# Warm-up matmuls on a preamble constant, and one weight block's load moved from the SP queue to the ACT queue

## The chip, the cores and the metric

The kernel runs on one core of a Trainium2 chip. The metric is the device time of one execution in microseconds (us); smaller is better. Times are medians of several executions. The profile adds one traced execution. Before the change the kernel takes 216.5 us, and most of that is one long stream of matmuls.

## The reference, cut to what matters

```python
def reference(A_x, ..., B_w1, B_b1, B_w2, B_b2, gate_w):
    x = A_x                                            # 2048 x 640, bf16
    g = _sigmoid((x * gate_w).sum(-1, keepdims=True))
    a = _A_ref(x, ...)                                 # a diagonal complex state-space scan
    b = _B_ref(x, B_w1, B_b1, B_w2, B_b2)              # gelu(x @ w1 + b1) @ w2 + b2; w1 is 640 x 1728
    return g * a + (1 - g) * b
```

The first work of TensorE (PE) is x @ w1 for the first 512 rows of x. It needs x transposed, 640 = 5 x 128 rows of it, and the five row blocks of w1. The five blocks are called k=0 to k=4 below.

## The kernel before

The kernel keeps a list of operations with priorities, and a small list scheduler turns them into one fixed order per engine. Loads are issued by the engine named in the call. `xtrans` is a transposing DMA (in this kernel only SP issues those), `w1load` a plain one of 128 rows of 2 KB.

```python
        w1load(0, "act", -101)
        xtrans(0, [0], 0, 1.27)          # x, block 0, transposed on the way in
        xtrans(0, [1, 2], 1, 1.27)       # blocks 1 and 2: "x's second transpose" below
        w1load(1, "sp", 2)               # "W1's second block" below: k=1
        w1load(2, "sp", 3)
        xtrans(0, [3, 4], 4, 1.27)
        w1load(3, "sp", 5)
        w1load(4, "sp", 6)
        ...
        # small parameter rows, 5 or 13 rows of 256 bytes, on ACT
        for i, (nm, (r0, src)) in enumerate(ROWS.items()):
            load(nm, "act", "l_" + nm, rows[r0:r0 + src.shape[0], :], src, [nm], prio=-100 + i, dur=0.4)
        load("b1b", "act", ..., prio=-96, dur=0.4)
        ...
        def f_warm():                    # dummy matmuls, so that PE's clock is up when the data comes
            t = None
            for _ in range(8):
                t = nc.tensor.matmul(PS[6][:, :], wz[:, 0:128], wz[:, :], start=True, stop=True)
            return inc("pe", t)
        op("warm", "pe", 3.2, ["wz"], [("bank", 6)], f_warm, prio=-1000)     # waits for a memset of wz by DVE
        ...
        def f_cols():                    # one PE transpose of the parameter rows
            return inc("pe", nc.tensor.transpose(psC, rows[:, :], ident[:, :]))
        op("cols", "pe", 0.3, list(ROWS) + ["b1b", "ident"], [("bank", 7)], f_cols, prio=7.5)
        ...
        def m1_first():                  # forty matmuls of 512 columns, k outermost: 8 column blocks for each k
            seq = [(k, jf) for k in range(KD) for jf in range(NW)]
            seq.remove((0, NW - 1))
            seq.insert(seq.index((1, NW - 1)), (0, NW - 1))
            for k, jf in seq:
                ... PS[jf] += W1sb[:, k, jf] ^T xT[0][:, k]     # reads ("xT", 0, k) and ("w1", k)
```

So PE does eight warm-up matmuls, seven matmuls of k=0, the transpose of the parameter rows, and then k=1, which needs x's second transpose and W1's second block.

Of the kernel before, what the change touches and what calls it, by code (L numbers as in the profile page):

```python
# [9 lines left out]
BF16 = mybir.dt.bfloat16  # L10
# [137 lines left out]
class Prog:  # L148
# [8 lines left out]
    def op(self, name, eng, dur, reads, writes, fn, prio=None, lat=0.0, after=()):  # L157
        deps = {}
        for k in reads:
            for w in self.last_w.get(k, ()):  # L160
                deps[w.idx] = w
        for k in writes:
            for w in self.last_w.get(k, ()):
                deps[w.idx] = w
            for r in self.last_r.get(k, ()):
                deps[r.idx] = r
        for a in after:
            deps[a.idx] = a
        deps = list(deps.values())
        E = self.E  # L170

        def run(eg, deps=deps, eng=eng, fn=fn):
            E.wait(eng, *[d.done for d in deps])
            return fn()

        it = self.sch.add(name, eng, dur, deps, run, prio=prio, lat=lat)
        for k in writes:
            self.last_w[k] = [it]
            self.last_r[k] = []
        for k in reads:  # L180
            self.last_r.setdefault(k, []).append(it)
        return it


def bass_gated_mix__ssm_conv_s5__dense_activation_gelu__prompt_kernel(
# [18 lines left out]
    _, S, D = A_x.shape  # L204
# [21 lines left out]
    with ExitStack() as es:  # L226

        def SB(name, shape, dt):
            return es.enter_context(nc.sbuf_tensor(name, list(shape), dt))
# [11 lines left out]
        cols = SB("cols", [128, 3 * KP + NF], FP32)  # L241
# [10 lines left out]
        ident = SB("ident", [128, 128], BF16)  # L252
# [33 lines left out]
        PS = [es.enter_context(nc.psum_tensor(f"ps{i}", [128, 512], FP32)) for i in range(8)]  # L286
# [13 lines left out]
        op = pr.op  # L300

        def inc(eng, ins):
            return E.inc(eng, ins, eng + "_s")
# [18 lines left out]
        def load(name, eng, sem, dst, src, writes, prio, dur=0.5, lat=2.5, reads=(), **kw):  # L322
            def fn():
                return dma_inc(eng, engines[eng].dma_start(dst, src), sem)
            return op(name, eng, dur, reads, writes, fn, prio=prio, lat=lat)
# [18 lines left out]
        def xtrans(q, ks, prio, dur):  # L344
            load_T(f"xT{q}_{ks[0]}", f"l_xT{q}_{ks[0]}", [(xT[q][:, ks[0]:ks[-1] + 1, :], x2[q * 512:(q + 1) * 512, ks[0] * 128:(ks[-1] + 1) * 128])],
                   [("xT", q, k) for k in ks], prio, dur)

        def w1load(k, eng, prio):
            load(f"w1_{k}", eng, f"l_w1{k}", W1sb[:, k, 0:FW], B_w1[k * 128:(k + 1) * 128, 0:FW], [("w1", k)], prio=prio, lat=2.6)
# [1 line left out]
        w1load(0, "act", -101)  # L351
        xtrans(0, [0], 0, 1.27)
        xtrans(0, [1, 2], 1, 1.27)
        w1load(1, "sp", 2)
        w1load(2, "sp", 3)
        xtrans(0, [3, 4], 4, 1.27)
        w1load(3, "sp", 5)
# [3 lines left out]
        ROWS = {"lre": (0, A_Lambda_re), "lim": (KP, A_Lambda_im), "ldt": (2 * KP, A_log_dt), "b1a": (3 * KP, B_b1[0:nmain])}  # L361
# [24 lines left out]

        op("const", "dve", 0.8, ["iota"], ["ident"], f_const, prio=-65)

        wz = SB("wz", [128, 512], BF16)

        def f_wz():
            return inc("dve", nc.vector.memset(wz[:, :], 0.0))  # L392

        op("wz", "dve", 0.35, (), ["wz"], f_wz, prio=-70)

        def f_warm():
            t = None
            for _ in range(8):
                t = nc.tensor.matmul(PS[6][:, :], wz[:, 0:128], wz[:, :], start=True, stop=True)  # L399
            return inc("pe", t)  # L400

        op("warm", "pe", 3.2, ["wz"], [("bank", 6)], f_warm, prio=-1000)

        def f_ones():
            inc("dve", nc.vector.memset(Gl[0][64:65, NF - 1, :], 1.0))
# [8 lines left out]
        def f_cols():  # L414
            return inc("pe", nc.tensor.transpose(psC, rows[:, :], ident[:, :]))  # L415

        op("cols", "pe", 0.3, list(ROWS) + ["b1b", "ident"], [("bank", 7)], f_cols, prio=7.5)

        def f_cols1():
            return inc("dve", nc.vector.tensor_copy(out=cols[:, :], in_=psC[:, 0:RT + 1]))  # L420
# [490 lines left out]
```

## Time and profile before

| | before |
|---|---|
| time, median of 3 (lowest to highest) | 216.51 us (216.29 to 216.52) |
| span of the profiled execution | 215.1 us |
| PE busy | 98% of the span |
| first warm-up matmul | 1.19 us |
| first matmul of k=0 / of k=1 | 4.58 / 7.57 us |
| last of the forty first matmuls starts | 14.71 us |

The page's first part gives the busy time of each engine, its share of the span, and the number of instructions.

```profile
PE 210.9 (98%) x1247; PEld 122.0 (57%) x1257; DVE 189.3 (88%) x262; ACT 99.0 (46%) x169; POOL 3.0 (1%) x11
```

PE is the limit, and its matmul work is fixed. A change can only gain or lose at the start, before the stream runs without a break. Here is PE's timeline of the first 17 us: start, length, engine, line, operation, tiles, and how many instructions the row merges. L399 is the warm-up, L601 the forty first matmuls, L415 the transpose of the parameter rows, L621 what follows.

```profile
1.19 3.60 PE L399 MATMUL ps<-wz 128*128 128x512 bf16 x8 [1.19 <-DVE wz L392]
4.58 2.89 PE L601 MATMUL ps<-xT,W1sb 128*128 128x512 bf16 x7
7.30 0.22 PE L415 MATMUL ps<-ident,rows 128*128 128x128 bf16 x1
7.57 7.52 PE L601 MATMUL ps<-xT,W1sb 128*128 128x512 bf16 x33
```

Seven matmuls of k=0 take 2.89 us and the next 33 take 7.52 us: starts are 0.427 us apart at first and 0.216 us apart later. PE starts at half its clock. (The page's row PEclk shows full clock from the first slice, so the half clock has to be read from this spacing; the trace's own clock record says full clock from 7.02 us.) The view of DMA issues, cut to the issues around 3.4 us, gives the time from issue to landing in its last column:

```profile
W1sb<-in_B_w_dram SPq DMA_DIRECT2D x1, 256.0 KB, 4.1
xT<-in_A_x_dram SPq DMA_TRANSPOSE x1, 3.8
```

W1's second block was issued at 3.40 us and landed at 7.48; x's second transpose was issued at 2.03 and landed at 5.83.

### The profile page before, as it was taken

The numbers are of one execution on the slowest core, as the hardware profiler recorded it, in microseconds if no ns is written. First come the engines' busy times: TensorE is split into PE (matmuls) and PEld (weight loads), VectorE is DVE, ScalarE is ACT, GpSimd is POOL, SyncE is SP. The second block draws the span as 40 slices with busy tenths as digits, with TensorE's granted clock in tenths as the row PEclk, the third lists the DMA queues.
The fourth block names the chain that finished last, engine by engine and source line by source line (L and its number), as shares of the span: only waits on it lengthen the run. The fifth ranks groups of instructions, "written<-read, shape, count | busy, mean of one in ns | idle before, by whom it ended". The sixth has DMA issues, their size and how long they took to land.

```text
span 215.1 us, 3184 instructions
## 1 busy us (share of the span) xinstructions
PE 210.9 (98%) x1247; PEld 122.0 (57%) x1257; DVE 189.3 (88%) x262; ACT 99.0 (46%) x169; POOL 3.0 (1%) x11
## 2 busy tenths in 40 slices
PE   7999999999999999999999999999999999999995
PEld 2344444444577775444467777444447777777773
DVE  3599999999999999999999999699999999959512
ACT  2469556675432224556642332556664233233220
POOL 1010000000000100000000010000000000000000
PEclk9999999999999999999999999999999999999999
DMA  6999799994000230100000022000000000000001
GB/s 132 293 274 200 196 382 227 215 216 101 0 0 34 43 140 0 34 0 0 3 0 30 0 84 103 30 3 0 0 0 3 8 35 21 30 30 30 34 30 30
DMA packets 30681, 16.09 MB, mean 75 GB/s; under 512 B 23948, under 2 KB 29772, under 8 KB 30668
## 3 DMA queue, kind: packets, MB, share of 16 engines
q1 hardware_dynamic: 30144, 14.32, 27.1%
q0 software_dynamic: 320, 1.31, 2.0%
q10 hardware_dynamic: 204, 0.27, 0.5%
q8 instruction: 10, 0.16, 0.3%
q14 instruction: 3, 0.02, 0.0%
HBM read 7.38 MB, written 2.62 MB: 47 GB/s over the span
## 4 chain that ended last, share of the span: by engine, by line
PE 98%; DVE 0%; issue 0%
PE ps L735 28%; PE ps L621 22%; PE ps L762 20%; PE ps L660 20%; PE ps L601 5%; PE ps L399 2%; PE ps L639 1%; DVE osb L795 0%; DVE wz L392 0%; PE ps L415 0%
## 5 line engine op out<-in xcount | busy, mean ns | idle before, releaser
L735 PE MATMUL ps<-W2sb,Gl 128*128 128x320 bf16 x448 | 63.6, 299 | 0.0
L735 PEld LDWEIGHTS ps<-W2sb,Gl 128*128 128x128 bf16 x448 | 43.8, 98 | 17.5
L621 PE MATMUL ps<-xT,W1sb 128*128 128x512 bf16 x214 | 47.3, 379 | 0.3
L762 PE MATMUL ps<-CT,H 128*128 128x320 bf16 x320 | 46.2, 299 | 0.0
L700 DVE TENSOR_TENSOR_SCAN W<-atab,V 128x1280 bf16<-128x1280 f32 x16 | 44.3, 2811 | 0.3
L660 PE MATMUL ps<-xT,BT 128*128 128x512 bf16 x196 | 43.1, 379 | 0.3 <-PE ps L639 0.2
L762 PEld LDWEIGHTS ps<-CT,H 128*128 128x128 bf16 x320 | 31.2, 98 | 12.6 <-issue 0.4
L743 ACT ACTIVATE E<-ps,g1col 128x320 bf16<-128x320 f32 x32 | 16.9, 527 | 43.8 <-PE ps L735 43.8
L628 ACT ACTIVATE Gl<-ps,cols 128x512 bf16<-128x512 f32 x44 | 29.8, 694 | 15.5 <-PE ps L621 15.5
L621 PEld LDWEIGHTS ps<-xT,W1sb 128*128 128x128 bf16 x220 | 21.5, 98 | 26.0
L660 PEld LDWEIGHTS ps<-xT,BT 128*128 128x128 bf16 x200 | 19.5, 98 | 23.5 <-issue 0.4
L669 ACT ACTIVATE U<-ps 128x512 bf16<-128x512 f32 x40 | 23.9, 597 | 18.3 <-PE ps L660 18.3
L773 ACT ACTIVATE E<-ps,gcol 128x320 bf16<-128x320 f32 x30 | 15.8, 527 | 24.2 <-PE ps L762 24.1
L465 DVE TENSOR_TENSOR osb<-xg,E 128x640 bf16<-128x640 bf16 x15 | 7.3, 486 | 9.0 <-ACT E L773 8.0
L781 DVE SCALAR_TENSOR_TENSOR xg<-xn,gcol,dsk 128x640 bf16<-128x640 bf16 x16 | 13.9, 883 | 0.4
L578 DVE SCALAR_TENSOR_TENSOR scr<-xn,gwb 128x640 bf16<-128x640 bf16 x16 | 13.2, 823 | 0.4
L465 DVE TENSOR_TENSOR V<-V,W 128x1280 bf16<-128x1280 bf16 x16 | 12.5, 821 | 0.3
L465 DVE TENSOR_TENSOR H<-H,V 128x1280 bf16<-128x1280 bf16 x16 | 12.5, 821 | 0.3
L465 DVE TENSOR_TENSOR V<-mr,U 128x2560 bf16<-128x2560 bf16 x8 | 11.9, 1489 | 0.2
L465 DVE TENSOR_TENSOR H<-c,W 128x2560 bf16<-128x2560 bf16 x8 | 11.9, 1490 | 0.1
L465 DVE TENSOR_TENSOR V<-s,W 128x2560 bf16<-128x2560 bf16 x8 | 11.9, 1485 | 0.0
L465 DVE TENSOR_TENSOR W<-mi,U 128x2560 bf16<-128x2560 bf16 x8 | 11.9, 1484 | 0.0
(77 smaller groups left out, 84.7 us busy)
## 6 DMA issues: line engine op xcount, KB each, us to landing
out_dram<-osb SPq DMA_DIRECT2D x15, 160.0 KB, 1.8
W2sb<-in_B_w_dram SPq DMA_DIRECT2D x1, 2080.0 KB, 11.1
xn<-in_A_x_dram SPq DMA_DIRECT2D x2, 640.0 KB, 6.0
xn<-in_A_x_dram POOLq DMA_DIRECT2D x2, 640.0 KB, 4.8
W1sb<-in_B_w_dram SPq DMA_DIRECT2D x4, 256.0 KB, 4.2
W1sb<-in_B_w_dram SPq DMA_DIRECT2D x1, 880.0 KB, 6.1
W1sb<-in_B_w_dram ACTq DMA_DIRECT2D x1, 256.0 KB, 2.7
gwb<-in_gate_w_dram SPq DMA_DIRECT2D x1, 160.0 KB, 5.6
```

The costliest lines, as they stand in the source:

```text
L465: return inc("dve", nc.vector.tensor_tensor(out=o, in0=a, in1=b, op=o_))
L578: t = inc("dve", nc.vector.scalar_tensor_tensor(out=scr[:, :], in0=xn[q % 2][:, c, :], scalar=1.0, in1=gwb[:, :], op0=ALU.mult, op1=ALU.mu ...
L621: t = nc.tensor.matmul(PS[bank][:, :], W1sb[:, k, jf * 128:(jf + 1) * 128], xT[q][:, k, :], start=(k == 0), stop=(k == KD - 1))
L628: return inc("act", nc.scalar.activation(Gl[q % 2][:, jf, :], PS[bank][:, :], ACT.Gelu_apprx_tanh, bias=b1col[:, jf:jf + 1]))
L660: t = nc.tensor.matmul(PS[bank][:, :], BT[:, ci, kd, k * 128:(k + 1) * 128], xT[q][:, kd, :], start=(kd == 0), stop=(kd == KD - 1))
L669: return inc("act", nc.scalar.activation(dst, src, ACT.Copy, scale=1.0 if ci == 0 else -1.0))
L700: t = inc("dve", nc.vector.tensor_tensor_scan(out=g[:, ci, :], data0=a, data1=v[:, ci, :], initial=0.0, op0=ALU.mult, op1=ALU.add))
L735: t = nc.tensor.matmul(PS[bank][:, 0:HALF], Gl[q % 2][0:n, jf, t4 * 128:(t4 + 1) * 128], W2sb[0:n, jf, cols], start=(jf == 0), stop=(jf == ...
L743: return inc("act", nc.scalar.activation(E1[c % NE][:, cols], PS[bank][:, 0:HALF], ACT.Copy, scale=g1col[:, c:c + 1]))
L762: t = nc.tensor.matmul(PS[bank][:, 0:HALF], H[b % NHB][:, ci, k, s * 128:(s + 1) * 128], CT[:, ci, k, cols], start=(i == 0), stop=(i == 2 ...
L773: return inc("act", nc.scalar.activation(E2[c % NE][:, cols], PS[bank][:, 0:HALF], ACT.Copy, scale=gcol[:, c:c + 1]))
L781: return inc("dve", nc.vector.scalar_tensor_tensor(out=xg[c % 2][:, :], in0=xn[q % 2][:, c % 4, :], scalar=gcol[:, c:c + 1], in1=dsk[:, :] ...
```

## The change

The intent: warm PE up earlier, and have W1's second block there earlier, so that the earlier clock can be used. The warm-up reads a constant that the preamble writes anyway, so it waits for no memset; nine matmuls fill the time that eight filled. W1's second block goes to the ACT queue, between the parameter rows. The two loads of b1's rows come later by that, so the transpose of the parameter rows is moved behind four more matmuls.

```diff
         w1load(0, "act", -101)
         xtrans(0, [0], 0, 1.27)
         xtrans(0, [1, 2], 1, 1.27)
-        w1load(1, "sp", 2)
+        w1load(1, "act", -97.5)
         w1load(2, "sp", 3)
...
-        wz = SB("wz", [128, 512], BF16)
-
-        def f_wz():
-            return inc("dve", nc.vector.memset(wz[:, :], 0.0))
-
-        op("wz", "dve", 0.35, (), ["wz"], f_wz, prio=-70)
+        one = nc.const_aps.tensor(1.0, [128, 1], BF16)

         def f_warm():
             t = None
-            for _ in range(8):
-                t = nc.tensor.matmul(PS[6][:, :], wz[:, 0:128], wz[:, :], start=True, stop=True)
+            for _ in range(9):
+                t = nc.tensor.matmul(PS[6][:, :], one.broadcast_to([128, 128]), one.broadcast_to([128, 512]), start=True, stop=True)
             return inc("pe", t)

-        op("warm", "pe", 3.2, ["wz"], [("bank", 6)], f_warm, prio=-1000)
+        op("warm", "pe", 3.6, (), [("bank", 6)], f_warm, prio=-1000)
...
-        op("cols", "pe", 0.3, list(ROWS) + ["b1b", "ident"], [("bank", 7)], f_cols, prio=7.5)
+        op("cols", "pe", 0.3, list(ROWS) + ["b1b", "ident"], [("bank", 7)], f_cols, prio=11.5)
```

## The prediction

> **What bounds the kernel.** TensorE. The chain of waits is 98% PE; after 9.5 us the timeline shows no PE wait above 0.2 us, only some missing records. The matmul work is fixed, so the change can only act on the first 15 us, until the fortieth W1 matmul of the first block is issued (14.7 us).
>
> **How that stretch goes now** (timeline, and the starts of single matmuls in the trace). The eight warm-up matmuls start at 1.19 us, behind a DVE memset (0.86 us, 0.27 long), and end at 4.6 us, just when the first transpose of x has landed (4.53). Matmuls with 512 columns start 0.427 us apart until about 7.02 us, then 0.216 us apart: half clock, then full clock. At 7.30 PE runs the transpose of the parameter rows, then waits about 0.2 us for W1's second row block (landed 7.48; k=1 starts 7.57). There is another 0.22 us wait at 9.3, within bank 7, which stays. The full-clock stretch in the trace lasts 208.21 us, from 7.02 to the end: 61.0 windows of 3.413 us. That agrees with the Trainium skill, "TensorE: Matmul & The Clock Gate", Part 1: the clock is judged in windows of 3.413 us and released after one busy window. On this grid the windows before are 0.20 to 3.61 and 3.61 to 7.02. The first had PE busy 2.42 of 3.41 us (71%, table by stretches), and did not release it.
>
> **What the change does.**
> 1. No memset to wait for: warm-up starts at about 0.78 us, 0.4 us earlier; nine at 0.427 still end at about 4.6. The first window is then 83% busy. If the threshold lies between 71% and 83%, full clock comes at 3.61 instead of 7.02. This is the whole question; I give it 60%.
> 2. W1's second block is issued by ACT at about 2.6 us instead of by SP at 3.40; I estimate landing near 6.0 instead of 7.48. SP's later loads are issued about 0.5 us earlier. b1's rows move 0.4 us later; the parameter transpose moves behind four more matmuls.
>
> **Critical path.** If released early: warm-up is over at 4.1, k=0 starts at 4.58 (x is the limit), takes 7 x 0.216, k=1 starts at about 6.2 when W1's second block is there, k=2 at 8.5, k=3 at 10.2 (W1's fourth block, 10.16 before, arrives a little earlier), the end of the forty at about 13.7 instead of 14.92. Gain about 1.2 us, time about 215.3. If not released early: only the 0.2 us wait for W1's second block goes, about 216.3. The DVE chain behind the parameter columns may start up to 0.9 us later, while PE gains; the tightest place is the second H tile (ready 71.1, read 74.1, 3 us of slack), so it shouldn't show.
>
> I set 215.5 us, range 214.9 to 216.5. Faster by over 2%: 0.01; within 2%: 0.97; slower: 0.02.
>
> **What would show it.** First warm-up matmul at 0.7 to 0.85 us. Spacing 0.216 us from about 3.6 us (released early) or from about 7.0 (not). A gap before the first W1 matmul in the first case. W1's second block landing before 6.5 us. k=1 starting without the 0.2 us wait. From the end of the forty matmuls on, the same timeline shifted by a constant.
>
> **What would make it wrong.** The windows may lie otherwise against the start of the kernel in other runs (the three times spread by only 0.23 us, so I take them as nearly fixed). Broadcast operands with step zero may be read more slowly than 0.427 us per matmul, and delay the first W1 matmul. The ACT-queue load shares DMA engines with the transposes of x and could delay them past 6.2 us. A later parameter transpose could hold up DVE more than I think.

## More of the kernel before

The next view gives, for stretches of 1 us, the length, the busy time of each engine with its count of instructions, the granted clock, the busy share of the 16 DMA engines (over 1 where packets are counted that end later) and GB/s.

```profile
4.00:5.00 1.00, 1.00 (x3) 0.16 (x2) 0.00 (x0) 1.00 (x1) 0.00 (x0) 1.00 1.28 230
5.00:6.00 1.00, 1.00 (x4) 0.44 (x3) 0.00 (x0) 0.01 (x1) 0.00 (x0) 1.00 0.66 178
6.00:7.00 1.00, 1.00 (x4) 0.31 (x3) 0.00 (x0) 0.00 (x0) 0.00 (x0) 1.00 0.94 333
7.00:8.00 1.00, 0.95 (x5) 0.32 (x4) 0.19 (x1) 0.21 (x1) 0.00 (x0) 1.00 1.28 131
8.00:9.00 1.00, 1.00 (x6) 0.49 (x5) 0.87 (x5) 0.68 (x2) 0.00 (x0) 1.00 1.23 290
```

## The result, and the profile after

The changed kernel is slower: 218.12 us (217.48 to 218.26, 4 runs) against 216.51 us (216.29 to 216.86). The ratio is 1.0067, with a 95% interval of 1.0043 to 1.0091. A ratio here and below is the mean time of one kernel's runs over that of the other's of the same rounds, so it isn't quite the ratio of the quoted medians. Executions over 1.5% slower than the fastest of the same kernel are left out of the means. The loss is under 2%, but it is clear of the noise, and it lies outside the predicted range.

PE's timeline of the changed kernel; L394 is the warm-up, L596 the forty matmuls, L410 the parameter transpose:

```profile
0.78 4.00 PE L394 MATMUL ps<-const-bfloat16-1.0 128*128 128x512 bf16 x9 [0.78 <-PEq L891]
5.64 1.68 PE L596 MATMUL ps<-xT,W1sb 128*128 128x512 bf16 x7 [0.87 <-DMA xT<-in_A_x_dram]
9.04 1.04 PE L596 MATMUL ps<-xT,W1sb 128*128 128x512 bf16 x4 [1.72 <-DMA xT<-in_A_x_dram]
10.04 0.22 PE L410 MATMUL ps<-ident,rows 128*128 128x128 bf16 x1
10.09 6.65 PE L596 MATMUL ps<-xT,W1sb 128*128 128x512 bf16 x29
```

The warm-up half does what it was meant to: it starts at 0.78 us, its broadcast operands take the usual 0.427 us a matmul, and the seven matmuls of k=0 now take 1.68 us, at full clock. But PE waits twice for x, 0.87 us before k=0 and 1.72 us before k=1 by the busy times. k=1 starts at 9.04 us instead of 7.57, and the fortieth matmul at 16.36 instead of 14.71. That is 1.65 us later, and the spans differ by the same 1.65 us (216.73 and 215.08): after the forty matmuls nothing is gained or lost. The chain of work that ended last shows where it hangs, with start, length and what ran or was waited for:

```profile
2.03 6.97 DMA xT<-in_A_x_dram
9.00 0.05 issue
9.04 1.04 PE ps L596 x4
```

The landing times of the loads issued around 2.6 us:

```profile
W1sb<-in_B_w_dram ACTq DMA_DIRECT2D x1, 256.0 KB, 6.2
xT<-in_A_x_dram SPq DMA_TRANSPOSE x1, 7.0
```

W1's second block is issued 0.8 us earlier than before (2.62) and lands 1.3 us later (8.79). x's second transpose is issued at the same 2.03 us and takes 7.0 us instead of 3.8, landing at 9.00. The packet records of the traces show the same: its 1,024 packets of 256 bytes began between 3.48 and 5.08 us before, and between 3.49 and 8.26 us here. (x's first transpose is later too, 5.60 instead of 4.53, but k=0 is through by 7.3 us, long before k=1 can start.) And in the same stretches as before the DMA engines are as busy and move much less:

```profile
4.00:5.00 1.00, 0.78 (x2) 0.00 (x0) 0.00 (x0) 0.80 (x1) 0.00 (x0) 1.00 1.13 143
5.00:6.00 1.00, 0.36 (x2) 0.21 (x3) 0.00 (x0) 0.48 (x1) 0.00 (x0) 1.00 0.80 115
6.00:7.00 1.00, 1.00 (x7) 0.39 (x4) 0.00 (x0) 0.00 (x0) 0.00 (x0) 1.00 1.25 152
7.00:8.00 1.00, 0.33 (x2) 0.00 (x0) 0.00 (x0) 0.00 (x0) 0.00 (x0) 1.00 1.17 162
8.00:9.00 1.00, 0.00 (x0) 0.00 (x0) 0.00 (x0) 0.00 (x0) 0.00 (x0) 1.00 0.85 183
```

The last column sums to 755 KB in these 5 us, against 1162 KB before, though the mean busy share is 1.04 here and 1.08 before. From 4 to 8 us a packet of 2 KB (a row of W1) took 253 ns on the mean, against 109 ns before, and 84 ns where copies run alone (9.2 to 10.5 us before, 10.0 to 11.3 us in the changed kernel).

So the theory (A): rows of W1 on ACT's queue and transposes of x on SP's queue are now in the DMA engines together, and both crawl. The rivals: (B) the new warm-up costs something; (C) any W1 block on ACT costs this, whenever it is issued; (D) the DMA engines are simply full, so only bytes count; (E) it is the changed order on SP; (F) SP and ACT share something in the making of descriptors (the orders that the DMA engines work from), rather than in the engines.

### The profile page after: what moved, and what is told of

Same layout as the page of the kernel before. It is cut to its first block, busy times and chain, and to the rows that moved or that the text cites. A ratio compares the mean times of both kernels' runs of the same rounds, so it can differ in the third digit from the quotient of the medians.

```text
span 216.7 us, 3195 instructions
## 1 busy us (share of the span) xinstructions
PE 211.0 (97%) x1258; PEld 121.7 (56%) x1258; DVE 188.8 (87%) x261; ACT 99.1 (46%) x169; POOL 3.0 (1%) x11
## 3 DMA queue, kind: packets, MB, share of 16 engines
HBM read 7.38 MB, written 2.62 MB: 46 GB/s over the span
## 4 chain that ended last, share of the span: by engine, by line
PE 95%; DMA 3%; SPq 1%; DVE 0%; issue 0%
PE ps L730 28%; PE ps L616 22%; PE ps L757 20%; PE ps L655 20%; PE ps L596 3%; DMA xT<-in_A_x_dram 3%; PE ps L634 1%; SPq L331 1%; DVE osb L790 0%; PE ps L410 0%
## 5 line engine op out<-in xcount | busy, mean ns | idle before, releaser
L616 PE MATMUL ps<-xT,W1sb 128*128 128x512 bf16 x220 | 48.1, 379 | 0.0
L655 PE MATMUL ps<-xT,BT 128*128 128x512 bf16 x200 | 43.8, 379 | 0.0
L596 PE MATMUL ps<-xT,W1sb 128*128 128x512 bf16 x40 | 9.3, 380 | 2.6 <-DMA xT<-in_A_x_dram 2.6
```

Source lines behind the costliest of these rows:

```text
L596: return inc("pe", nc.tensor.matmul(PS[jf][:, :], W1sb[:, k, jf * 128:(jf + 1) * 128], xT[0][:, k, :], start=(k == 0), stop=(k == KD - 1)))
L616: t = nc.tensor.matmul(PS[bank][:, :], W1sb[:, k, jf * 128:(jf + 1) * 128], xT[q][:, k, :], start=(k == 0), stop=(k == KD - 1))
L655: t = nc.tensor.matmul(PS[bank][:, :], BT[:, ci, kd, k * 128:(k + 1) * 128], xT[q][:, kd, :], start=(kd == 0), stop=(kd == KD - 1))
```

## The experiments

All kernels gave correct results. Times are us, with the number of runs. "SP-first" and other names are explained at their run.

### The two halves alone

The warm-up half alone, with W1's second block back on SP and the parameter transpose at its old place:

```diff
-        w1load(1, "act", -97.5)
+        w1load(1, "sp", 2)
...
-        op("cols", ..., prio=11.5)
+        op("cols", ..., prio=7.5)
```

> The warm-up half of the change alone: nine warm-up matmuls on the preamble's constant; W1's second row block stays on SP, the parameter transpose stays behind seven matmuls. Theory A (the loss is the ACT-queue load, which mixes with the transposes of x): x's second transpose lands near 5.8 us and W1's second block near 7.5 us as before, k=1 starts at 7.5 to 7.6 us whatever the clock does, and the time is that of before, 216.3 to 216.7 us. Theory B (the warm-up costs: broadcast operands, or ones, or the earlier start): about 218 us. What my prediction said of an early clock alone: up to 1.2 us faster; theory A says it is worth nothing here, since W1's second block is what k=1 waits for.

Measured: 216.5 (216.24 to 216.86, 6 runs), ratio 0.9998 (0.9978 to 1.0018). The warm-up neither costs nor gains, so B falls. Its timeline shows where an earlier start goes:

```profile
0.78 4.00 PE L394 MATMUL ps<-const-bfloat16-1.0 128*128 128x512 bf16 x9 [0.78 <-PEq L891]
4.75 2.50 PE L596 MATMUL ps<-xT,W1sb 128*128 128x512 bf16 x7
7.08 0.22 PE L410 MATMUL ps<-ident,rows 128*128 128x128 bf16 x1
7.79 7.52 PE L596 MATMUL ps<-xT,W1sb 128*128 128x512 bf16 x33 [0.48 <-issue]
```

PE is through k=0 and the parameter transpose a little earlier and then stands idle for 0.48 us, until W1's second block lands at 7.70. The slow clock of before had been hidden behind this load.

The load half alone: the diff's other lines on the old kernel, eight warm-up matmuls on the zeroed tile.

> The other half alone: W1's second block on ACT between the parameter rows, parameter transpose behind eleven matmuls; the old eight warm-up matmuls on the zeroed tile. Theory A: x's second transpose lands near 9.0 us and W1's second block near 8.8 us as in the changed kernel (5.8 and 7.5 before), k=1 starts near 9.0, time 217.5 to 218.3 us. Theory B: the time of before, about 216.5 us.

Measured: 216.93 in the middle of five runs, but these go from 215.68 to 218.58, and there was one execution of 791.71 us. Ratio 1.0023 (0.998 to 1.0066): inconclusive as a time. The profile fell on the execution of 791.71 us, in which matmuls of 512 columns are some 0.84 us apart to the end: PE at about a quarter of its clock, from the warm-up on (more on it at the end). Its loads are of use all the same: x's second transpose landed at 8.76 us and W1's second block at 8.51, as theory A said. The spread was not expected, and is taken up below.

### The suspected cost by itself

The warm-up half alone, plus a load on ACT of 256 KB that nothing computes with, at the very place where the changed kernel loads W1's second block. (The diffs here leave out one more line: a much later operation on ACT names the copy among its inputs.)

```diff
+        w1copy = SB("w1copy", [128, FW], BF16)
+        load("w1copy", "act", "l_w1copy", w1copy[:, :], B_w1[0:128, 0:FW], ["w1copy"], prio=-97.5, lat=2.6)
         w1load(1, "sp", 2)
...
-        op("cols", ..., prio=7.5)
+        op("cols", ..., prio=11.5)
```

> The suspected cost by itself: the kernel with the warm-up half alone (W1's second block on SP, behind x's second transpose, as before), but ACT also loads 256 KB of W1 that nothing computes with, at the place where the changed kernel loads W1's second block; parameter transpose behind eleven matmuls. Theory A: the idle copy alone delays x's second transpose from 5.7 to 8 to 9 us and the first by up to 1 us; W1's second block follows at about 9.5, k=1 starts at 9 to 9.8 us, time 217.5 to 218.7. Rival D (the DMA engines are full and only the bytes count): 256 KB are about 0.65 us of DMA at the 400 GB/s seen later, so W1's second block lands near 8.3 us and the time is at most 217.2. Rival E (what harms is the order on SP, W1's third block directly behind x's second transpose): no change, 216.5.

Measured: 219.32 (218.4 to 221.02, 6 runs), ratio 1.0135 (1.0102 to 1.0168), more than expected. The landing times of its loads issued at 3.4 us and of the transpose before them, and its DMA rates:

```profile
W1sb<-in_B_w_dram SPq DMA_DIRECT2D x1, 256.0 KB, 5.5
xT<-in_A_x_dram SPq DMA_TRANSPOSE x1, 6.4
```

```profile
4.00:5.00 1.00, 0.47 (x3) 0.11 (x2) 0.00 (x0) 0.80 (x1) 0.00 (x0) 1.00 1.06 193
5.00:6.00 1.00, 1.00 (x6) 0.49 (x5) 0.00 (x0) 0.48 (x1) 0.00 (x0) 1.00 1.05 92
6.00:7.00 1.00, 0.50 (x3) 0.00 (x1) 0.00 (x0) 0.00 (x0) 0.00 (x0) 1.00 1.14 113
```

The idle copy alone moves x's second transpose from 3.7 us after its issue (5.69, in the warm-up half alone) to 6.4 us after it (8.38). W1's second block, behind it on SP's queue, lands at 8.92, and k=1 starts at 9.01 us. SP's own order is that of before, so E falls. 256 KB at the 374 to 402 GB/s that these engines reach from 9 to 12 us in the kernel before are 0.7 us; the delay is 2.7 us, so D falls. Some of its runs are slower still. The slowest (221.02) has a mean granted clock of 0.984, so part of its excess is the clock; why was not traced.

Meant as the control: the same copy, issued by ACT at 8.6 us, so that it would run beside plain loads of SP only, with the parameter transpose at its old place.

```diff
-        load("w1copy", "act", ..., prio=-97.5, lat=2.6)
+        load("w1copy", "act", ..., prio=-948.5, lat=2.6, reads=["amag"])
```

> Control for the idle copy: the same 256 KB by ACT, but issued at about 8.6 us, when SP's ring holds plain loads of W1 (until about 12.5 us), parameter transpose behind seven matmuls. Theory A: copies beside copies cost only their bytes, W1's last loads land up to 0.7 us later (the remainder near 13.7 instead of 13.1, needed at 14.9), no matmul waits for them, time as with the warm-up half alone, 216.2 to 216.9 us. Rival (any second queue costs): a loss of 1 us or more.

Measured: 216.42 (216.3 to 216.92, 4 runs), ratio 1.0003 (0.9985 to 1.002). No matmul is delayed, so the expectation held for the time. But the run is not the control that it was meant to be. The first packet of the copy began only at 12.13 us, 3.5 us after the issue, when SP's plain loads were nearly through and the transposes of the next matrix (BT) had begun (11.97). The copy ran among those until 16.27 and landed at 16.76, and BT's landing moved from 16.82 us (warm-up half alone) to 20.12. Nothing needs that matrix so early. So this is a second case of a copy from ACT beside transposes from SP, with a delay of 3.3 us, and not a case of copies beside copies; for that see SP-first below. And the late first packet is a hint at F: what ACT issued did not start until what SP had issued earlier was under way.

### The same load at other times and from other queues

The changed kernel with W1's second block on ACT directly behind the first, at 1.19 us instead of 2.62:

```diff
-        w1load(1, "act", -97.5)
+        w1load(1, "act", -100.5)
```

> The changed kernel with W1's second block issued on ACT directly behind the first (at about 1.2 us instead of 2.6), before the parameter rows. Theory A: its packets run mostly from 2.5 to 4 us, against the first transpose of x; what is mixed is less, because both W1 blocks are mostly through before the second transpose begins. I expect the first transpose at 5 to 5.6 us, the second at 6 to 7, k=1 at 6.2 to 7.2 us, time 215.2 to 216.2. Rival C (any row block on ACT beside SP's transposes costs the same, whenever it is issued): about 218 us. If the parameter rows, now about 0.4 us later, were the limit, the parameter transpose would come after 10 us as in the changed kernel.

Measured: 215.87 (215.75 to 216.27, 6 runs), ratio 0.9971 (0.9953 to 0.999): a little faster than before. C falls: on the same queue, 1.4 us earlier, the load costs no time. x's first transpose landed at 5.30, W1's second block at 5.03, the second transpose at 6.23. The load's packets ran from 3.24 to 4.30 us, and for only 0.6 us of that beside packets of transposes (none ran from 3.66 to 4.13).

The changed kernel with W1's second block on SP in front of x's first transpose ("SP-first"):

```diff
-        w1load(1, "act", -97.5)
+        w1load(1, "sp", -1)
```

> The changed kernel with W1's second block issued on SP before the first transpose of x; nothing large is on the ACT queue beside transposes. Theory A: no mixing of packets of the two kinds over two queues; W1's second block lands before 4.5 us, the first transpose about 0.5 us later than before (5.1), the second near 6.4, k=1 at 6.4 to 6.8 us, time 215.2 to 216.0 us. Rival D (the DMA engines are simply full, so that moving W1's second block forward pushes the transposes back by as much): k=1 stays near 7.5 us or later, time 216.5 or more.

Measured: 215.79 (215.7 to 216.12, 6 runs), ratio 0.9968 (0.995 to 0.9986). With the run before it this is the best version found (the two can't be told apart), and it beats both kernels: 0.3% faster than before by the ratio, and about 1.0% faster than the changed kernel (0.9968 against 1.0072, each against the kernel before). Its timeline:

```profile
5.32 2.55 PE L596 MATMUL ps<-xT,W1sb 128*128 128x512 bf16 x11 [0.69 <-DMA xT<-in_A_x_dram]
7.70 0.22 PE L410 MATMUL ps<-ident,rows 128*128 128x128 bf16 x1
7.76 6.66 PE L596 MATMUL ps<-xT,W1sb 128*128 128x512 bf16 x29
```

PE waits once, until x's first transpose lands at 5.27, and then never again: k=0 flows into k=1 at full clock. The price of loading W1's second block first is about 0.7 us on the first transpose (4.53 before). Two rivals that were not named fall here as well. The moved parameter transpose is in this kernel too, so it is not what costs. And two plain loads on two queues do not crawl: W1's first block on ACT and its second on SP had their packets from 1.76 to 4.00 us, 512 KB in 2.2 us, where the first block took 1.3 us in the kernel before.

A third place, on SP between x's two transposes:

```diff
-        w1load(1, "act", -97.5)
+        w1load(1, "sp", 0.5)      # x's transposes have 0 and 1
```

> A version meant to be better: W1's second block on SP between x's first and second transpose, with the new warm-up, parameter transpose behind eleven matmuls. x's first transpose should land at 4.5 to 4.7 us (5.3 with the block in front of it), W1's second block near 5.5, the second transpose near 6.7. [...]k=1 at 6.5 to 7.3 us, time 215.3 to 216.2; against SP-first (215.8) it is a close call.

Measured: 216.13 (215.73 to 216.42, 6 runs), ratio 0.9984 (0.9968 to 1.0). The first transpose landed at 4.28 us, W1's second block at 5.68, the second transpose at 6.51, all near the expectation. In the profiled execution PE was slow until 6.65 us, and k=1 therefore started only at 7.17.

From POOL's queue, meant to have its packets where the changed kernel has them:

```diff
-        w1load(1, "act", -97.5)
+        load("w1_1", "pool", "l_w11", W1sb[:, 1, 0:FW], B_w1[128:256, 0:FW], [("w1", 1)], prio=-50, lat=2.6, reads=["ident"])
```

> Is it ACT's queue, or any second queue? The changed kernel with W1's second block issued by POOL once the identity tile is ready (about 2.9 us), so that its packets come at about 4 us, as in the changed kernel. Theory A (packets of copies and of transposes mixed in the DMA engines): x's second transpose lands at 7.5 to 9.5 us, W1's second block after 7.5, time 217 to 219. Rival F (ACT and SP share a descriptor generator, and that is what is held up): the second transpose stays near 5.8 us, W1's second block lands near 6.5 to 7, k=1 near 7, time 215.5 to 216.5.

Measured: 215.99 (215.85 to 216.66, 6 runs), ratio 0.9978 (0.9959 to 0.9998). The expectation of A missed the time, and that of F missed the landing: x's second transpose landed at 7.47 us, 1.6 us later than before, where F said 5.8, and W1's second block at 7.33. So a load that ACT doesn't issue also delays the transpose, and F can't be the whole cause. How much of it F is stays open, because the timing failed: POOL's first packet began at 5.20 us, when 1,458 of the 1,536 packets of x's first two transposes had begun, while ACT's in the changed kernel began at 4.36, after 703. The load from POOL also ran as 64 packets of 4 KB, those from ACT and SP as 128 of 2 KB. The smaller delay can come from either, and no run varied one alone.

### The changed kernel and the load half again

The spread of the load half asked for more runs of both. First the changed kernel, unaltered:

> The changed kernel once more, unaltered, for the spread of its time: the act-only kernel spread from 215.7 to 218.6 us, while the changed one has so far given 217.5 to 218.3 in four runs. If the mixing of the two queues' packets depends on small offsets (theory A with luck in it), I expect some runs near 215.5 to 216 and most near 217.5 to 218.3. If it is fixed, all runs are at 217.4 to 218.3.

Measured: 217.99 (217.76 to 218.39, 6 runs), ratio 1.0072 (1.0057 to 1.0086), with x's second transpose at 8.85 us: fixed, not luck. Then both on one chip:

> The act-only kernel again, since its first job gave 215.7 to 218.6 us and its one profile fell on an execution at a quarter of the clock. Theory A with luck in it (the mixing depends on small offsets of the two queues): again two groups, near 216 and near 218, and the profile shows x's second transpose near 6 us in a fast one or near 9 in a slow one. If the spread was that chip's or that job's: all runs at 217.4 to 218.4.

> The changed kernel on the same chip as the act-only one. If the luck is in the ACT-queue load alone, it must show here too: some runs near 215.5 to 216. If all are at 217.5 to 218.4 again, while the act-only kernel spreads, then the two kernels differ in something that I haven't named.

Measured: the load half 217.42 (215.77 to 218.32, 6 runs), ratio 1.0025 (0.9989 to 1.0061), again in groups, with two of six near 215.8; its profiled execution is one of 218.32 us, with the second transpose at 9.31. The changed kernel 218.19 (217.62 to 219.54, 6 runs), ratio 1.0082 (1.0056 to 1.0108). The 219.54 us are explained in part by the clock: a mean granted clock of 0.992 of full means 1.6% of the span at half clock, 3.5 us, about one window of 3.4 us (the windows are explained further down). Where in the run this was, no trace shows: in the profiled execution PE kept its full clock through the window with the hole in its work (1.68 us busy from 5.47 to 8.88).

Five more looks at the load half were to catch a fast execution in a profile:

> A look at the act-only kernel, for a profile of a fast execution. If it is fast (below 216.3 us): theory A says that x's second transpose lands before 7 us in it and k=1 starts before 7.3. If it is slow (above 217): the second transpose lands after 8.3 us.

> As the look before it: fast with the second transpose before 7 us, or slow with it after 8.3 us. A fast execution with the second transpose still at 8.3 or later would contradict theory A.

> As the two looks before it; with the chance of a fast execution at 4 in 11, the three together catch one about three times in four.

> The act-only kernel once more. Fast executions (below 216.3 us) should have x's second transpose before 7 us and k=1 before 7.3; slow ones (above 217) after 8.3 us. I expect one fast execution in three; a profile of one is a matter of luck.

> The same as the run before it, for a second chance of a profile of a fast execution and for the share of fast ones: one in three expected, none would say that the first two jobs were unusual.

Measured: 217.9, 217.8 and 218.11 (one run each), then 216.88 (215.87 to 218.87, 4 runs) and 218.29 (216.09 to 218.53, 4 runs). The profiled execution was slow in all five, with the second transpose at 8.74 to 9.78 us. Leaving out the one of 791.71 us, 7 of 22 executions of the load half were below 216.3 us, none of them profiled, and 0 of 16 of the changed kernel. Every profiled execution, seven of the load half and three of the changed kernel, shows the slow loads. All seven of the load half were slow or at a quarter of the clock, while 7 of its other 16 were fast, so being profiled may itself matter; that was not tested. Why the load half escapes at times and the changed kernel never did stays open; no run shows it.

### What the warm-up half is worth once the data is there

SP-first with the old warm-up (eight matmuls behind the memset):

```diff
-        w1load(1, "sp", 2)
+        w1load(1, "sp", -1)
...
-        op("cols", ..., prio=7.5)
+        op("cols", ..., prio=11.5)
```

> SP-first with the old warm-up (eight matmuls behind the memset at 1.19 us): what is the warm-up half worth once W1's second block is no longer waited for? [...]SP-first with the new warm-up gave 215.7 to 216.1 us. I expect 215.7 to 216.6 us here, median 216.0, with more spread.

> A look at SP-first with the old warm-up, for one of its slow executions (218 us, 2 in 6). If the clock is to blame, matmuls are 0.427 us apart until later than 7.1 us, or again after a wait; if the loads are, the second transpose of x or W1's fourth block lands 2 us later than the 6.2 and 10.7 us of its first profile.

Measured: 216.42 (215.87 to 218.41, 6 runs), ratio 1.0016 (0.9981 to 1.0052), and 218.53 in the look. The spread was larger than expected: two of six near 218, where SP-first with the new warm-up stays within 215.7 to 216.12. A slow one:

```profile
1.19 3.60 PE L399 MATMUL ps<-wz 128*128 128x512 bf16 x8 [1.19 <-DVE wz L392]
5.62 4.87 PE L601 MATMUL ps<-xT,W1sb 128*128 128x512 bf16 x11 [0.83 <-DMA xT<-in_A_x_dram]
```

Eleven matmuls take 4.87 us, where they took 2.55: the clock stayed at half until 10.46 us, with x's second transpose landed at 6.53. The view by stretches explains it; its columns here are length, PE's busy time and count, and then clock, DMA share and GB/s. The stretches are the windows of 3.413 us counted back from the moment of full clock.

```profile
0.22:3.63 3.41, 2.44 (x6) 1.00 0.49 136
3.63:7.05 3.42, 2.59 (x7) 1.00 1.14 236
7.05:10.46 3.41, 3.41 (x11) 1.00 1.03 280
```

Neither of the first two windows was busy enough, the second because of the hole in which PE waited for x. The kernel before and the changed one:

```profile
0.20:3.61 3.41, 2.42 (x6) 1.00 0.49 120
3.61:7.02 3.41, 3.41 (x9) 1.00 0.90 231
```

```profile
2.06:5.47 3.41, 2.72 (x7) 1.00 0.84 168
```

And the load half, full clock from 10.10 us:

```profile
3.27:6.69 3.42, 2.69 (x7) 1.00 0.97 101
6.69:10.10 3.41, 2.85 (x8) 1.00 1.09 209
```

2.69 us of busy time in a window did not release the clock, 2.72 did, and so did 2.85; 2.42, 2.44 and 2.59 did not. By this measure (which counts the modelled tail of a matmul) the threshold is at about 79% of a window. And the windows lie differently against the start of the kernel in every execution: full clock came at 3.88 us in one kernel with the new warm-up, at 4.12, 4.33, 4.43, 5.47, 6.26 and 6.65 in others.

## Why the prediction was wrong

It named 215.5 us, in a range of 214.9 to 216.5, and 218.12 was measured. Point by point:

- "First warm-up matmul at 0.7 to 0.85 us": right, 0.78. Nine matmuls at 0.427 us: right. Early release of the clock in the profiled execution: right in outcome, full clock by the first matmul of k=0 (5.47 us), but partly by luck: it was the window from 2.06 to 5.47 that released it (2.72 us busy, hardly more than the 2.69 us that did not in another run), and not one from 0.20 to 3.61 as the fixed windows would have had it.
- "This is the whole question" (whether the clock is released early): wrong. The warm-up half alone has a ratio of 0.9998, because k=1 waits for W1's second block until 7.7 us in any case. The prediction had seen the landing at 7.48 and a wait of 0.2 us, and took it as settled by its point 2 that the load would be earlier. So the clock looked like the only open term; the slow clock and the load were two limits of the same length.
- The step that failed is point 2 of the prediction, "I estimate landing near 6.0 instead of 7.48", with "k=1 starts at about 6.2 when W1's second block is there". W1's second block landed at 8.79, x's second transpose at 9.00 instead of 5.83, and k=1 started at 9.04, 2.8 us later than predicted. This one term turns the gain of 1.2 us into a loss of 1.65 us. The risk was named at the end ("shares DMA engines with the transposes of x and could delay them past 6.2 us"), but it was given no size and no weight in the range. The idle copy shows the size: 2.7 us on that transpose for 256 KB. That a load from ACT, under way beside x's second transpose, is the cause is shown: taken away (the warm-up half alone), added by itself (the idle copy), and moved in time or to SP (SP-first and its neighbours). Whether the two meet in the DMA engines (A) or partly already in the making of descriptors (F) is not shown.
- "The three times spread by only 0.23 us, so I take them as nearly fixed" (the windows): wrong. They lie anywhere. The likely reason that the three times were alike is that in the kernel before PE waits for the load, which hides the clock; this was argued, not tested.
- "From the end of the forty matmuls on, the same timeline shifted by a constant": right, 1.65 us at the fortieth matmul and at the end. The parameter transpose came 2.7 us later, not up to 0.9, but all of PE's later work came 1.65 us later too, and no further loss is seen in the spans.

The gain that the prediction expected does exist for the most part: SP-first has it without the mixing, 0.8 us by the medians of the runs made side by side (215.79 against 216.61).

The Trainium skill says in "DMA: Bandwidth & Descriptors", section "Issuing engines are not separate DMA queues", that DMAs issued by different engines run on the same 16 DMA engines and interleave, so that a second issuing engine only saves issue time. This trace agrees: in the changed kernel packets of both queues ran beside each other from 4.36 to 8.19 us, and the saved time was 0.8 us of issue (2.62 against 3.40). The section "Queues, rings and completion order" adds that a DMA engine takes turns between the queues that have work, a packet at a time; a packet there is a group of descriptors, and no run here shows whether it is what the profile counts as one. The slow stretch from 4 to 8 us, with 2 KB packets at 253 ns, doesn't contradict that, but the trace doesn't show the turns themselves, and in the late idle copy ACT's load had no packet at all for 3.5 us while SP's loads ran.

## What to carry to other kernels

Before speeding up a busy stretch, look up when the data of the next one lands: where that is the same moment, the gain is nothing until both move. Don't start a plain load on a second queue while a transposing DMA that somebody waits for is in flight; put it in front of the transposes, where the DMA engines are still idle, and look at GB/s, not at the busy share, to see whether the engines make headway. A start whose time depends on where the clock's windows fall needs more than three runs, and a hole in PE's first work can cost a whole window of half clock.

## What the Trainium skill lacked or had wrong

- "DMA: Bandwidth & Descriptors", rules for kernel authors, says of safety that "A transpose next to ordinary DMAs needs nothing". It doesn't say what it costs: here 256 KB of plain load on ACT's queue beside a transpose on SP's moved the transpose's landing from 3.7 to 6.4 us after its issue (the idle copy), and in the changed kernel the engines moved 755 KB in 5 us instead of 1162 KB at about the same busy share. W1's second block on SP in front of the transposes did not slow the kernel (ratio 0.9968).
- The same page has no figure for copies that directly follow a transpose. In the kernel before, packets of 2 KB took 109 ns on the mean from 4 to 8 us (352 ns for the first 16 behind x's second transpose), and 84 ns later, among copies alone. It isn't so each time: behind x's third transpose in the changed kernel they took 84 ns from the first, so a fixed cost of the turn is not shown.
- "TensorE: Matmul & The Clock Gate", Part 1, says that the windows of 3.413 us are free-running and that the clock is released after a busy one. Both agree with the runs: in all twelve traces that have a clock record the full-clock stretch is 61.0 or 62.0 windows long, and it began anywhere from 3.88 to 10.46 us. It gives no threshold: here 2.69 us of PE busy time in a window did not release the clock and 2.72 us did, about 79%.
- The same page mentions executions that stay at a quarter of the clock for 50 us and more. Here one execution of the load half stayed there to its end: 791.71 us instead of some 217, matmuls of 512 columns some 0.84 us apart. The granted clock in the profile said 1.00 for it, so the spacing is what to look at. It was one of 23 executions of that kernel, and nothing shows its cause.
